# Turned blocks of a token mixer stored by row quarter first and channel chunk second

## The chip, the cores and the metric

The kernel runs on one core of a Trainium2 chip. The metric is the device time of one execution in microseconds (us), the median of several.

## The reference, cut to what matters

```python
def _attn_ref(x, weight):                       # x 8 x 4096 x 192, weight 8 heads x 7 taps
    w = softmax(weight)                         # over the taps
    out = np.einsum('hk,bskhg->bshg', w, x_unf) # causal convolution over 7 rows, per head
    return out.reshape(B, S, D)

def _moe_ref(x, w_tok1, w_tok2, w_ch1, w_ch2):
    xt = x.transpose(0, 2, 1)
    h = np.maximum(xt @ w_tok1, 0.0) @ w_tok2   # mixes the 4096 rows through 256
    u = x + h.transpose(0, 2, 1)
    h2 = np.maximum(u @ w_ch1, 0.0) @ w_ch2     # mixes the 192 channels through 1536
    return u + h2
```

All is float32. The kernel splits every float32 operand into a high and a low part (`hi`, `lo`) and multiplies high by high, high by low and low by high.

## The kernel before, in words

The eight batches are worked off in five groups: two single batches, then three pairs (`GROUPS`, L14). A group passes through two stages. The first (convolution, then the row mixer down to 256) runs as background work, in pieces that a planner puts between the instructions of the group ahead. The second takes eight tiles of 512 rows one after the other: `mix2` (L1030) mixes a tile's rows back up and adds, giving u; u is turned so that channels lie on partitions; `channel1` (matmuls in `channel1_mm`, L1214) multiplies by `w_ch1`, and `channel2` (L1290) by `w_ch2`, whose results two additions per 128 rows (L1304, L1305) take out of PSUM. For a pair, channel1 and channel2 run twice per tile, once for each batch of it.

The turning is what the change touches. VectorE's transpose (L1051 for a pair, L1044 for a single batch) turns blocks of 32 x 32 only, in place on the partitions. The other half of the work, bringing block (row quarter i, channel group q) to the partitions of q, is an exchange: `blocks_sent` issues sixteen DMAs (L1125) of 48 KB between two SBUF tiles, eight on SP's queue and eight on POOL's. Each goes from 32 partitions to 32 partitions. It is split by a channel dimension of three, `ND`, the chunks of 64 channels: a partition holds 12 blocks of 32 channels (6 for a single batch), numbered chunk first, then quarter.

What the exchange brings is then parted. For a pair, `parted` does so in this order, with c over the three chunks:

- ScalarE copies the arrived values to `own_hi` (L1157), which rounds them to the high part, and VectorE copies the lower 64 partitions of that over to the upper 64 of `swapped[0]` (L1158);
- VectorE subtracts: `own_lo` = arrived - `own_hi` (L1162), three times;
- ScalarE copies the lower 64 partitions of `own_lo` to the upper 64 of `swapped[1]` (L1165), three times;
- POOL sends the other halves by two DMAs (L1167).

`swapped[1]` is `other[:, 1]`, the very tile in which the arrived values lie, so L1165 overwrites what L1162 reads:

```python
        swapped = other[:, 0], other[:, 1]                          # L1152
            v = f32(other[:, 1, c]).rearrange("p (i j e) -> p j i e", i=NQ, e=QB)
            nc.vector.tensor_tensor(out=lo, in0=v, in1=f32(hi), op=ALU.subtract)
            nc.scalar.copy(out=swapped[1][high, c], in_=f32(own[1][low, c]))
```

The first block of channel1 is 18 matmuls, 9 products for each half of the array: three with the high weights and high values, three with the low weights and high values, three with the high weights and low values. In each triple one product per chunk c. The upper half's last three read `swapped[1]`, chunk by chunk. For a single batch, `parted_single` has one copy (L1135) and one subtraction in place (L1141) per chunk, and no swapped tile.

There are 29 exchanges: 5 for the second single batch (tile `own_lo`), 12 in the middle of the run for pairs (into `other` from `own_hi`, here called the open ones: the next tile's channel1 comes right after the channel2 under which they run) and 12 later ones for pairs (from the tile `raw`), which are issued one channel1 and channel2 earlier and here called the early ones.

Order: SP and POOL each issue their DMAs strictly in the program's order, and a framework adds waits on semaphores where two instructions touch the same bytes. Loads of the input for the convolution (L726, 128 partitions x 14 pieces of 384 bytes, 672 KB each) stand on SP's queue as well.

Of the kernel before, what the change touches and what calls it, by code (L numbers as in the profile page):

```python
# [148 lines left out]
def conv_mixer_kernel(ctx: ExitStack, tc: tile.TileContext, x, weight, w_tok1, w_tok2, w_ch1, w_ch2, out):  # L149
    nc = tc.nc  # L150
    B, S, D = x.shape
# [24 lines left out]
    def f32(ap):  # L176
        return ap.bitcast(F32)
# [829 lines left out]
    def mix2(gi, q, t2, u, z):  # L1007
# [15 lines left out]
        for step, js in enumerate(SHARES):  # L1023
            for j in js:
                if step < 2:
                    pss[j] = ps_x.tile([P, TT], F32, name="ps_x")
            for i, (kc, r, v, m) in enumerate(prods):
                for k, j in enumerate(js):
                    ks = half_rows(k)
                    nc.tensor.matmul(  # L1030
                        out=pss[j][:, :m], lhsT=lhs(kc, r, j)[ks], rhs=v[ks], start=step < 2 and i == 0,
                        stop=step > 1 and i == len(prods) - 1,
                    )
            if step < 2:
                part_ends(pss[js[1]])
            bg.fg(570 if nb == 1 else 1060, 0 if step < 2 else 1320 if nb == 1 else 900, 200 if z is None or step < 2 else -1e6)
            for j in sorted(js) if step > 1 else ():
                ps = pss[j]
                if nb == 1:
                    two, one = flat(u)[:, j, 0], flat(u)[:, j, 1]  # L1040
                    nc.vector.tensor_tensor(out=one, in0=ps[:, D:2 * D], in1=one, op=ALU.add)
                    nc.vector.tensor_tensor(out=two, in0=ps[:, :D], in1=one, op=ALU.add)
                    if z is not None:
                        nc.vector.transpose(  # L1044
                            out=z[:, :D // QB, j * QB:(j + 1) * QB], in_=two.rearrange("p (n e) -> p n e", e=QB)
                        )
                        bg.dve += 380
                else:
                    v = ps[:, :W].rearrange("p (b c d) -> p c b d", b=nb, d=D2)
                    nc.vector.tensor_tensor(out=u[:, j], in0=v, in1=u[:, j], op=ALU.add)  # L1050
                    nc.vector.transpose(  # L1051
                        out=z[:, :, j * QB:(j + 1) * QB],
                        in_=u[:, j].rearrange("p c b d -> p (c b d)").rearrange("p (n e) -> p n e", e=QB),
                    )
                    bg.dve += 580

# [20 lines left out]
    def transposed_halves(u, abc):  # L1077
# [28 lines left out]

        return {(1, 5): lambda: turn(0), (2, 3): parts}

    def blocks_sent(z, nb, pool, name):

        if nb == 1:
            other = own_tile("lo")
            blocks = z[:, :D // QB].rearrange("p (c n) t -> p n c t", n=NQ // 2)
            home = other
        else:
            other = pool.tile([P, 2, ND, TT], F32R, name=name)
            blocks = z.rearrange("p (c n) t -> p n c t", n=NQ)
            home = other[:, 1]  # L1120
        for k in range(NQ):
            for q in range(NQ):
                i = (q + k) % NQ
                queue = nc.gpsimd if q % 2 else nc.sync
                queue.dma_start(  # L1125
                    out=f32(home[q * QB:(q + 1) * QB, :, i * P:(i + 1) * P]),
                    in_=blocks[i * QB:(i + 1) * QB, q % (2 * nb)],
                )
        return other

    def parted_single(lo):
        own = own_tile("hi")
        for c in range(ND):
            v = f32(lo[:, c])
            nc.scalar.copy(  # L1135
                out=own[:, c].rearrange("p (j i e) -> p j i e", i=NQ, e=QB),
                in_=v.rearrange("p (i j e) -> p j i e", i=NQ, e=QB),
            )
            bg.fg(0, 700, 0)
            blocks = "p (i j e) -> p i j e"  # L1140
            nc.vector.tensor_tensor(  # L1141
                out=lo[:, c].rearrange(blocks, i=NQ, e=QB), in0=v.rearrange(blocks, i=NQ, e=QB),
                in1=f32(own[:, c]).rearrange("p (j i e) -> p i j e", i=NQ, e=QB), op=ALU.subtract,
            )
        own = own, lo.rearrange("p c (i j e) -> p c j i e", i=NQ, e=QB), range(ND)
        return [(own, own)]

    def parted(other):
# [3 lines left out]
        swapped = other[:, 0], other[:, 1]  # L1152
        low, high = slice(0, D2), slice(D2, P)
        for c in range(ND):
            v = f32(other[:, 1, c]).rearrange("p (i j e) -> p j i e", i=NQ, e=QB)
            hi, lo = (o[:, c].rearrange("p (j i e) -> p j i e", i=NQ, e=QB) for o in own)
            nc.scalar.copy(out=hi, in_=v)  # L1157
            nc.vector.tensor_copy(out=swapped[0][high, c], in_=f32(own[0][low, c]))  # L1158
        for c in range(ND):
            v = f32(other[:, 1, c]).rearrange("p (i j e) -> p j i e", i=NQ, e=QB)  # L1160
            hi, lo = (o[:, c].rearrange("p (j i e) -> p j i e", i=NQ, e=QB) for o in own)
            nc.vector.tensor_tensor(out=lo, in0=v, in1=f32(hi), op=ALU.subtract)  # L1162
        bg.dve += 3600
# [429 lines left out]
```

## Time and profile before

| | |
|---|---|
| three runs | 2046.98, 2049.78, 2050.49 us, median 2049.78 |
| the profiled execution, its own time | 2046.99 us |
| its span, first to last instruction | 2045.2 us |
| TensorE (PE) busy | 2018.5 us, 99% of the span |
| VectorE (DVE), ScalarE (ACT), GpSimd (POOL) busy | 68%, 38%, 11% |
| mean granted TensorE clock | 0.997 of full speed |
| the 16 DMA engines | 128 GB/s on average |

A busy share counts a matmul that stands in the pipeline behind a late operand as busy, so the 99% says that TensorE is never left for long, not that every product comes at its own pace. The pace is read from the starts of matmuls in the timeline.

### The profile page before, as it was taken

How to read it: one execution, taken by the hardware profiler on the slowest of the kernel's cores; microseconds unless marked ns; L12 is line 12 of the kernel's file. 1: busy time of each engine (PE TensorE's matmuls, PEld its weight loads, DVE VectorE, ACT ScalarE, POOL GpSimd, SP SyncE). 2: the span in 40 equal slices, each digit the busy share in tenths (PEclk: the TensorE clock that was granted, in tenths of full speed). 3: DMA queues.
4: the chain of work that ended last, by engine and by line, in shares of the span. 5: the costliest groups of instructions: out<-in, count | busy, mean ns of one | idle time of the engine just before them, and what ended most of it. 6: DMA issues, size and time to landing. Idle time of an engine off the chain costs nothing.

```text
span 2045.2 us, 52230 instructions
## 1 busy us (share of the span) xinstructions
PE 2018.5 (99%) x22404; PEld 1896.1 (93%) x22404; DVE 1398.0 (68%) x2747; ACT 782.5 (38%) x1582; POOL 219.1 (11%) x385
## 2 busy tenths in 40 slices
PE   9999999999999999999999999999999999999999
PEld 9889999998989889999998999899999999999998
DVE  8888989888758978847965895544455444554443
ACT  5677534433333434323333342322333223333222
POOL 0000000021211011101111101111110111101110
PEclk9999999999999999999999999999999999999999
DMA  9956445656455676436664375332332333323320
GB/s 303 311 159 206 138 131 177 174 142 191 140 143 133 174 181 158 106 100 138 168 161 116 92 186 138 84 79 54 74 80 72 83 84 76 79 73 84 79 53 16
DMA packets 285238, 262.67 MB, mean 128 GB/s; under 512 B 189136, under 2 KB 233040, under 8 KB 285008
## 3 DMA queue, kind: packets, MB, share of 16 engines
q1 hardware_dynamic: 263280, 185.27, 33.9%
q0 software_dynamic: 21728, 74.08, 12.7%
q8 instruction: 176, 2.88, 0.6%
q14 instruction: 54, 0.44, 0.1%
HBM read 146.31 MB, written 71.30 MB: 106 GB/s over the span
## 4 chain that ended last, share of the span: by engine, by line
PE 80%; DVE 7%; DMA 6%; ACT 3%; SPq 2%; issue 1%; POOL 1%; DVEq 0%; ACTq 0%; POOLq 0%
PE ps_x L1214 35%; PE ps_x L1290 31%; PE ps_x L1030 6%; PE ps_a L861 5%; DVE xc L738 2%; SPq L1125 2%; PE ps_x L1246 1%; DMA dec_raw<-in_moe_w_tok_dram 1%; DMA other<-own_hi 1%; DMA raw<-in_x_dram 1%; DVE hl L1273 1%; DVE own_lo L1162 1%; ACT own_hi L1157 1%; DMA dec_raw<-in_moe_w_ch_dram 1%; POOL other L1125 1%
## 5 line engine op out<-in xcount | busy, mean ns | idle before, releaser
L1290 PE MATMUL ps_x<-w,hh 64*128 64x384 f32 x5856 | 861.5, 356 | 0.3 <-DVE hl L1273 0.3
L1290 PE MATMUL ps_x<-w,hl 64*128 64x192 f32 x5856 | 831.9, 247 | 0.9 <-DVE hl L1273 0.8
L1290 PEld LDWEIGHTS ps_x<-w,hl 64*128 64x128 f32 x5856 | 696.2, 188 | 1.7 <-DVE hl L1273 1.4
L1290 PEld LDWEIGHTS ps_x<-w,hh 64*128 64x128 f32 x5856 | 691.9, 184 | 1.5 <-DVE hl L1273 0.8
L1272 ACT ACTIVATE hh<-ps_x 128x512 fp32r<-128x512 f32 x744 | 404.1, 594 | 551.7 <-PE ps_x L1214 551.5
L1273 DVE SCALAR_TENSOR_TENSOR hl<-ps_x,hh 128x512 fp32r<-128x512 f32 x744 | 477.0, 685 | 196.3 <-ACT hh L1272 195.5
L738 DVE SCALAR_TENSOR_TENSOR xc<-raw,cw,xc 128x384 f32<-128x384 f32 (+1 forms) x768 | 383.1, 562 | 14.4 <-ACT xc L736 14.3
L1214 PE MATMUL ps_x<-other,w_hi 64*128 64x512 f32 x1296 | 353.4, 393 | 3.7 <-ACT other L1165 1.2
L1214 PE MATMUL ps_x<-own_hi,w_hi 64*128 64x512 f32 x1440 | 342.4, 398 | 7.2 <-ACT own_hi L1135 6.2
L1214 PE MATMUL ps_x<-own_lo,w_hi 64*128 64x512 f32 x1440 | 336.9, 393 | 0.0
L1214 PE MATMUL ps_x<-own_hi,w_lo 64*128 64x512 f32 x1440 | 332.6, 390 | 0.0
L1214 PEld LDWEIGHTS ps_x<-other,w_hi 64*128 64x128 f32 x1296 | 235.0, 184 | 36.7 <-ACT other L1165 12.5
L1304 DVE TENSOR_TENSOR osb<-ps_x,u 128x192 f32<-128x192 f32 x244 | 85.6, 351 | 241.8 <-PE ps_x L1290 241.8
L1214 PEld LDWEIGHTS ps_x<-own_lo,w_hi 64*128 64x128 f32 x1440 | 222.1, 185 | 20.0 <-DVE own_lo L1162 1.2
L1214 PEld LDWEIGHTS ps_x<-own_hi,w_lo 64*128 64x128 f32 x1440 | 222.6, 186 | 18.1
L1214 PEld LDWEIGHTS ps_x<-own_hi,w_hi 64*128 64x128 f32 x1440 | 215.7, 186 | 25.3 <-ACT own_hi L1135 7.7
L1214 PE MATMUL ps_x<-other,w_lo 64*128 64x512 f32 x648 | 182.8, 388 | 0.0
L423 ACT COPY ps_x<-seen 1x2 f32<-1x2 f32 x198 | 30.0, 152 | 365.0 <-PE ps_x L1290 315.3
L1030 PE MATMUL ps_x<-h,t 64*128 64x384 f32 (+1 forms) x1408 | 134.2, 327 | 2.2 <-DVE hl L1273 1.6
L1030 PEld LDWEIGHTS ps_x<-h,t 64*128 64x128 f32 x1408 | 127.6, 184 | 5.5 <-DVE hl L1273 3.4
L1214 PEld LDWEIGHTS ps_x<-other,w_lo 64*128 64x128 f32 x648 | 119.4, 184 | 10.7
L861 PE MATMUL ps_a<-xhl,t 64*128 64x384 f32 x1056 | 120.8, 336 | 2.7 <-DMA t<-t1p 2.7
(178 smaller groups left out, 1834.6 us busy)
## 6 DMA issues: line engine op xcount, KB each, us to landing
raw<-in_x_dram SPq DMA_DIRECT2D x56, 672.0 KB, 8.6
t<-t2d SPq DMA_DIRECT2D x64, 512.0 KB, 5.8
u<-xcd SPq DMA_DIRECT2D x62, 384.0 KB, 7.7
xcd<-xc POOLq DMA_DIRECT2D x28, 768.0 KB, 7.9
t<-t1p SPq DMA_DIRECT2D x32, 512.0 KB, 5.0
out_dram<-osb POOLq DMA_DIRECT2D x34, 384.0 KB, 2.7
out_dram<-osb SPq DMA_DIRECT2D x29, 384.0 KB, 2.8
t2d<-stage SPq DMA_DIRECT2D x16, 512.0 KB, 4.6
```

The lines of the kernel that those rows point to most:

```text
L423: nc.scalar.copy(out=ps[0:1, TT - 2:TT], in_=seen)
L738: nc.vector.scalar_tensor_tensor(out=dst, in0=src, scalar=cw[:, h, k:k + 1], in1=dst, op0=ALU.mult, op1=ALU.add)
L861: nc.tensor.matmul(out=accs[kcs[k]][:, :nb * D], lhsT=w[ks], rhs=x[ks], start=first and step == 0 and i == 0, stop=last and step == 1 and ...
L1030: nc.tensor.matmul(out=pss[j][:, :m], lhsT=lhs(kc, r, j)[ks], rhs=v[ks], start=step < 2 and i == 0, stop=step > 1 and i == len(prods) - 1,)
L1125: queue.dma_start(out=f32(home[q * QB:(q + 1) * QB, :, i * P:(i + 1) * P]), in_=blocks[i * QB:(i + 1) * QB, q % (2 * nb)],)
L1157: nc.scalar.copy(out=hi, in_=v)
L1162: nc.vector.tensor_tensor(out=lo, in0=v, in1=f32(hi), op=ALU.subtract)
L1214: nc.tensor.matmul(out=ps, lhsT=w1[w][rows, t[h][2][c], p * P:(p + 1) * P], rhs=t[h][v][rows, c], start=a and n == 0, stop=z and n == len( ...
L1272: nc.scalar.activation(out=h["hh", f], in_=ps, func=AF.Relu)
L1273: nc.vector.scalar_tensor_tensor(out=h["hl", f], in0=ps, scalar=0.0, in1=f32(h["hh", f]), op0=ALU.max, op1=ALU.subtract)
L1290: nc.tensor.matmul(out=pss[j][:, :m], lhsT=h[part, f][ks, j * P:(j + 1) * P], rhs=w2[ks, f, :m], start=step < 2 and n == 0 and part == "hh ...
L1304: nc.vector.tensor_tensor(out=rows(osb[:, j]), in0=rows(ps[:, :D]), in1=tokens(u, i)[:, j], op=ALU.add)
```

## The change

The turned blocks are numbered quarter first, then chunk, so that the three chunks of one block pair lie next to each other, both in the tile that is sent and in the tile that arrives. A transfer thus has one run of 1536 bytes per partition in place of three of 512. All readers and writers of these tiles use views (`by_rows`, `by_blocks_of`) that follow the new numbering: the transposes, ScalarE's copies to the high part, and the subtractions. What `swapped[1]` means is not changed: chunk c at columns 512c to 512c + 511.

```diff
@@ -1042,15 +1042,16 @@
                     nc.vector.tensor_tensor(out=two, in0=ps[:, :D], in1=one, op=ALU.add)
                     if z is not None:
                         nc.vector.transpose(
-                            out=z[:, :D // QB, j * QB:(j + 1) * QB], in_=two.rearrange("p (n e) -> p n e", e=QB)
+                            out=by_rows(z, 1)[:, :, :, j * QB:(j + 1) * QB],
+                            in_=two.rearrange("p (c q e) -> p c q e", c=ND, e=QB),
                         )
                         bg.dve += 380
                 else:
                     v = ps[:, :W].rearrange("p (b c d) -> p c b d", b=nb, d=D2)
                     nc.vector.tensor_tensor(out=u[:, j], in0=v, in1=u[:, j], op=ALU.add)
                     nc.vector.transpose(
-                        out=z[:, :, j * QB:(j + 1) * QB],
-                        in_=u[:, j].rearrange("p c b d -> p (c b d)").rearrange("p (n e) -> p n e", e=QB),
+                        out=by_rows(z, nb)[:, :, :, j * QB:(j + 1) * QB],
+                        in_=u[:, j].rearrange("p c b d -> p c (b d)").rearrange("p c (q e) -> p c q e", e=QB),
                     )
                     bg.dve += 580
 
@@ -1106,43 +1107,47 @@
 
         return {(1, 5): lambda: turn(0), (2, 3): parts}
 
+    def by_rows(z, nb):
+        return z[:, :nb * D // QB].rearrange("p (q c) t -> p c q t", c=ND)
+
+    def by_blocks_of(t):
+        return t.rearrange("p c t -> p (c t)").rearrange("p (i c t) -> p i c t", i=NQ, c=ND)
+
     def blocks_sent(z, nb, pool, name):
 
 
 
         if nb == 1:
             other = own_tile("lo")
-            blocks = z[:, :D // QB].rearrange("p (c n) t -> p n c t", n=NQ // 2)
             home = other
         else:
             other = pool.tile([P, 2, ND, TT], F32R, name=name)
-            blocks = z.rearrange("p (c n) t -> p n c t", n=NQ)
             home = other[:, 1]
+        blocks = z[:, :nb * D // QB].rearrange("p (q c) t -> p q (c t)", c=ND)
+        home = home.rearrange("p c t -> p (c t)").rearrange("p (i n) -> p i n", i=NQ)
         for k in range(NQ):
             for q in range(NQ):
                 i = (q + k) % NQ
                 queue = nc.gpsimd if q % 2 else nc.sync
                 queue.dma_start(
-                    out=f32(home[q * QB:(q + 1) * QB, :, i * P:(i + 1) * P]),
+                    out=f32(home[q * QB:(q + 1) * QB, i]),
                     in_=blocks[i * QB:(i + 1) * QB, q % (2 * nb)],
                 )
         return other
 
     def parted_single(lo):
-        own = own_tile("hi")
+        own, blocks = own_tile("hi"), by_blocks_of(lo)
         for c in range(ND):
-            v = f32(lo[:, c])
+            v = f32(blocks[:, :, c])
             nc.scalar.copy(
-                out=own[:, c].rearrange("p (j i e) -> p j i e", i=NQ, e=QB),
-                in_=v.rearrange("p (i j e) -> p j i e", i=NQ, e=QB),
+                out=own[:, c].rearrange("p (j i e) -> p i j e", i=NQ, e=QB), in_=v.rearrange("p i (j e) -> p i j e", e=QB)
             )
             bg.fg(0, 700, 0)
-            blocks = "p (i j e) -> p i j e"
             nc.vector.tensor_tensor(
-                out=lo[:, c].rearrange(blocks, i=NQ, e=QB), in0=v.rearrange(blocks, i=NQ, e=QB),
+                out=blocks[:, :, c].rearrange("p i (j e) -> p i j e", e=QB), in0=v.rearrange("p i (j e) -> p i j e", e=QB),
                 in1=f32(own[:, c]).rearrange("p (j i e) -> p i j e", i=NQ, e=QB), op=ALU.subtract,
             )
-        own = own, lo.rearrange("p c (i j e) -> p c j i e", i=NQ, e=QB), range(ND)
+        own = own, blocks.rearrange("p i c (j e) -> p c j i e", e=QB), range(ND)
         return [(own, own)]
 
     def parted(other):
@@ -1152,12 +1157,12 @@
         swapped = other[:, 0], other[:, 1]
         low, high = slice(0, D2), slice(D2, P)
         for c in range(ND):
-            v = f32(other[:, 1, c]).rearrange("p (i j e) -> p j i e", i=NQ, e=QB)
+            v = f32(by_blocks_of(other[:, 1])[:, :, c]).rearrange("p i (j e) -> p j i e", e=QB)
             hi, lo = (o[:, c].rearrange("p (j i e) -> p j i e", i=NQ, e=QB) for o in own)
             nc.scalar.copy(out=hi, in_=v)
             nc.vector.tensor_copy(out=swapped[0][high, c], in_=f32(own[0][low, c]))
         for c in range(ND):
-            v = f32(other[:, 1, c]).rearrange("p (i j e) -> p j i e", i=NQ, e=QB)
+            v = f32(by_blocks_of(other[:, 1])[:, :, c]).rearrange("p i (j e) -> p j i e", e=QB)
             hi, lo = (o[:, c].rearrange("p (j i e) -> p j i e", i=NQ, e=QB) for o in own)
             nc.vector.tensor_tensor(out=lo, in0=v, in1=f32(hi), op=ALU.subtract)
         bg.dve += 3600
```

The order of the instructions on every engine is the same as before. Two places show what moves. The first is ScalarE's queue at the first open exchange, with what each instruction waits for: the copies to `own_hi` (L1157, L1162 in the change), the copies of `own_lo` into `other` (L1165, L1170 in the change), then channel1's activations (L1272, L1277). Before:

```order
L423 COPY ps_x<-seen 1x2 [waits DVE_49,PE_49] x4
L1157 CAST own_hi<-other 128x512 [waits DMAHW0_49,DMASW7_49,DMAHW1_49,DMASW6_49,DMAHW2_49,DMASW5_49,DMAHW3_49,DMASW4_49,DMAHW4_49,DMASW3_49,DMAHW5_49,DMASW2_49,DMAHW6_49,DMASW1_49,DMAHW7_49,DMASW0_49,DVE_49]
L1157 CAST own_hi<-other 128x512 x2
L1165 CAST other<-own_lo 64x512 [waits DVE_49,Activation_49] x3
L1272 ACTIVATE hh_8659<-ps_x 128x512 [waits PE_49] x4
```

And in the change:

```order
L423 COPY ps_x<-seen 1x2 [waits DVE_49,PE_49] x4
L1162 CAST own_hi<-other 128x512 [waits DMAHW0_49,DMASW7_49,DMAHW1_49,DMASW6_49,DMAHW2_49,DMASW5_49,DMAHW3_49,DMASW4_49,DMAHW4_49,DMASW3_49,DMAHW5_49,DMASW2_49,DMAHW6_49,DMASW1_49,DMAHW7_49,DMASW0_49,DVE_49]
L1162 CAST own_hi<-other 128x512 x2
L1170 CAST other<-own_lo 64x512 [waits DVE_49,Activation_49]
L1170 CAST other<-own_lo 64x512 x2
L1277 ACTIVATE hh_8659<-ps_x 128x512 [waits PE_49] x4
```

Before, each of the three copies has a wait of its own for VectorE; now the first waits for VectorE once and the two behind it wait for nothing more, so the first one's wait covers them all.

The second place is SP's queue at the two open exchanges that start at 978.97 and 1036.28 us in the trace. Before:

```order
L1125 DMA other<-own_hi 32x3x128 x8
L726 DMA raw_13404<-in_x_dram 128x14x96 x2
L726 DMA raw_13409<-in_x_dram 128x14x96 x2
L1336 DMA out_dram<-osb 128x768
L978 DMA t_13487<-t2d 128x2x512 x2
L988 DMA u<-xcd_77 128x12x64 x2
L1125 DMA other<-own_hi 32x3x128 x8
L726 DMA raw_14285<-in_x_dram 128x14x96 x2
```

And in the change:

```order
L1132 DMA other<-own_hi 32x384 x8
L726 DMA raw_13404<-in_x_dram 128x14x96 x2
L726 DMA raw_13409<-in_x_dram 128x14x96 x2
L1341 DMA out_dram<-osb 128x768
L978 DMA t_13487<-t2d 128x2x512 x2
L988 DMA u<-xcd_77 128x12x64 x2
L1132 DMA other<-own_hi 32x384 x8
L726 DMA raw_14285<-in_x_dram 128x14x96 x2
```

Nothing changes places; the exchange's DMAs have two dimensions in place of three. Input loads stand right behind the exchange on SP's queue here, as at seven of the twelve open exchanges; at four an output store stands there, at one a load of `t1p`.

## Rows read from the trace of the kernel before

**Rows 1.** The page: the span, TensorE's busy time, and by 40 equal slices the granted TensorE clock in tenths.

```profile
span 2045.2 us, 52230 instructions
PE 2018.5 (99%) x22404; PEld 1896.1 (93%) x22404; DVE 1398.0 (68%) x2747; ACT 782.5 (38%) x1582; POOL 219.1 (11%) x385
PEclk9999999999999999999999999999999999999999
```

**Rows 2.** Busy time by stretch (us from the span's start: length, then PE, PEld, DVE, ACT and POOL busy with instructions, granted clock, DMA share, GB/s): the open exchanges and the early ones.

```profile
590.00:1320.00 730.00, 722.62 (x8145) 667.35 (x8143) 543.38 (x1037) 258.69 (x538) 90.62 (x155) 1.00 0.54 138
1331.00:1990.00 659.00, 659.00 (x7632) 630.11 (x7630) 328.28 (x635) 200.97 (x420) 72.22 (x132) 1.00 0.30 75
```

**Rows 3.** Groups of instructions by line, with busy us and mean ns, then the idle time of the engine before them by releaser.

```profile
L1165 ACT CAST other<-own_lo 64x512 fp32r<-64x512 f32 x54 | 32.8, 618 | 31.2 <-DVE own_lo L1162 31.2
L1157 ACT CAST own_hi<-other 128x512 fp32r<-128x512 f32 x54 | 29.9, 620 | 46.0 <-DMA other<-own_hi 46.0
...
L1162 DVE TENSOR_TENSOR own_lo<-xc,own_hi 128x512 fp32r<-128x512 f32 x18 | 11.4, 687 | 2.2 <-issue 2.2
...
L1157 ACT CAST own_hi<-xc 128x512 fp32r<-128x512 f32 x18 | 10.0, 627 | 0.0
```

**Rows 4.** ScalarE's copies into `swapped[1]` (L1165): who waited for them, in us and times.

```profile
  PEld ps_x L1214: 12.5, 30
  PE ps_x L1214: 1.2, 6
```

**Rows 5.** Timeline of ScalarE from 1043 us, the open exchange issued at 1036: start, length, line, operation, count, in brackets the idle time before and its releaser.

```profile
1043.80 1.66 ACT L1157 CAST own_hi<-other 128x512 fp32r<-128x512 f32 x3 [4.00 <-DMA other<-own_hi]
1047.04 1.82 ACT L1165 CAST other<-own_lo 64x512 fp32r<-64x512 f32 x3 [1.58 <-DVE own_lo L1162]
```

**Rows 6.** The same stretch on VectorE.

```profile
1046.25 1.90 DVE L1162 TENSOR_TENSOR own_lo<-other,own_hi 128x512 fp32r<-128x512 f32 x3 [0.34 <-DMA raw<-in_x_dram]
...
1049.11 0.36 DVE L1305 TENSOR_TENSOR osb<-ps_x,osb 128x192 f32<-128x192 f32 x1
```

**Rows 7.** The same stretch on TensorE: the first block of channel1 and the start of the second. Rows with `other` are the upper half of the array, with `own` the lower.

```profile
1046.06 0.41 PE L1214 MATMUL ps_x<-own_hi,w_hi 64*128 64x512 f32 x1
...
1047.22 0.39 PE L1214 MATMUL ps_x<-other,w_lo 64*128 64x512 f32 x1
...
1047.44 0.39 PE L1214 MATMUL ps_x<-other,w_lo 64*128 64x512 f32 x1
...
1047.71 0.50 PE L1214 MATMUL ps_x<-other,w_hi 64*128 64x512 f32 x1
...
1048.31 0.50 PE L1214 MATMUL ps_x<-other,w_hi 64*128 64x512 f32 x1
...
1048.91 0.50 PE L1214 MATMUL ps_x<-other,w_hi 64*128 64x512 f32 x1
1049.01 0.46 PE L1214 MATMUL ps_x<-own_hi,w_hi 64*128 64x512 f32 x1
1049.52 0.50 PE L1214 MATMUL ps_x<-other,w_hi 64*128 64x512 f32 x1
1049.53 0.50 PE L1214 MATMUL ps_x<-own_hi,w_hi 64*128 64x512 f32 x1
1049.86 0.39 PE L1214 MATMUL ps_x<-other,w_hi 64*128 64x512 f32 x1
```

**Rows 8.** Timelines of SP's and POOL's queues, the open exchange at 1036 (input loads behind it) and the one at 1093 (none behind it), and when ScalarE starts on the latter.

```profile
1036.28 5.08 SPq L1125 DMA_DIRECT2D other<-own_hi  x8
1041.46 1.49 SPq L726 DMA_DIRECT2D raw<-in_x_dram  x2
...
1036.85 4.35 POOL L1125 DMA_DIRECT2D other<-own_hi  x8 [17.37 <-DVE xc L738]
...
1093.78 5.10 SPq L1125 DMA_DIRECT2D other<-own_hi  x8
...
1094.35 4.35 POOL L1125 DMA_DIRECT2D other<-own_hi  x8 [18.31 <-ACT ps_x L423]
...
1101.10 1.14 ACT L1157 CAST own_hi<-other 128x512 fp32r<-128x512 f32 x2 [3.79 <-DMA other<-own_hi]
```

**Rows 9.** The exchange's DMAs (L1125) from 1093 to 1101 us: issue durations in ns (min/median/max), and us from the start of the issue to the landing.

```profile
L1125 SPq DMA_DIRECT2D other<-own_hi x8: 591/598/604, 1093.8 to 1098.3; - x8
L1125 POOL DMA_DIRECT2D other<-own_hi x8: 548/548/573, 1094.3 to 1098.2; - x8
...
DMA to landing us min/median/max: 1.9/2.1/2.4
```

**Rows 10.** Issue durations in ns of DMAs with one run per partition: two kinds on SP, one on POOL.

```profile
L1336 SPq DMA_DIRECT2D out_dram<-osb x33: 332/357/10315, 424.5 to 2042.6; - x33
...
L1439 SPq DMA_DIRECT2D t2d<-stage x16: 319/328/2213, 111.2 to 248.5; - x16
...
L1167 POOL DMA_DIRECT2D other<-own_lo x18: 517/523/530, 608.1 to 1981.8; - x18
```

**Rows 11.** Landings of the exchange's DMAs (L1125) from 444 to 457 us: an exchange of a single batch that was issued while two input loads (issued from 440.7 us) were in flight.

```profile
DMA to landing us min/median/max: 3.7/5.5/8.2
```

**Rows 12.** TensorE's waits: engine and line, releaser, us in total, times, longest.

```profile
PE ps_x L1214 <- ACT own_hi L1135: 6.2, 2, 4.5
```

**Rows 13.** An early exchange: its issue on SP (L1125), ScalarE's copies after it, and TensorE's first product that reads it.

```profile
1335.16 5.11 SPq L1125 DMA_DIRECT2D xc<-raw  x8
...
1361.86 1.82 ACT L1165 CAST xc<-own_lo 64x512 fp32r<-64x512 f32 x3 [1.60 <-DVE own_lo L1162]
...
1371.28 0.41 PE L1214 MATMUL ps_x<-xc,w_hi 64*128 64x512 f32 x1
```

**Rows 14.** Groups by line again: VectorE's subtraction with plain views (L1273), and the transposes of the open exchanges.

```profile
L1273 DVE SCALAR_TENSOR_TENSOR hl<-ps_x,hh 128x512 fp32r<-128x512 f32 x744 | 477.0, 685 | 196.3 <-ACT hh L1272 195.5
...
L1051 DVE STREAM_TRANSPOSE own_hi<-u 128x384 f32<-128x384 f32 x48 | 27.8, 579 | 1.6
```

## The prediction

> **What bounds the kernel now.** TensorE does: busy for 2018.5 of 2045.2 us at the full clock [rows 1], and without any gap over the stretch of the early exchanges [rows 2]. A change elsewhere therefore counts only where TensorE waits, or keeps time because an operand is late. The groups by line show where that is at the exchanges. Before the copies to `own_hi` (L1157) of the open exchanges ScalarE sits idle for 46.0 us, and the DMAs end it; before those of the early ones it sits idle for 0.0 [rows 3]. So only the open exchanges arrive when they are already wanted. Who waits at their end is told by the view of L1165: 30 weight loads and 6 matmuls [rows 4], 36 in all, which is 12 open exchanges times 3 chunks. At every open exchange, each of the three copies into `swapped[1]` is what TensorE's next product waits for.
>
> The waits add up to 13.7 us only because a matmul that is held in the pipeline counts as busy. The timeline shows the real loss; I take the exchange of 1036 us. The arrived data start ScalarE at 1043.80, the copies L1165 run from 1047.04 to 1048.86 [rows 5], the subtractions before them from 1046.25 [rows 6], and the upper half's last three products start at 1047.71, 1048.31 and 1048.91 [rows 7], 0.60 apart like the copies, each 0.05 after its copy's end. Undisturbed products are 0.22 to 0.23 apart (1047.22, 1047.44) [rows 7]. Nine of them from 1046.06 would end at 1048.1. Instead the second block's first product starts at 1049.01, and its upper half at 1049.52, held by the PSUM buffer that L1305 frees at 1049.47 [rows 6]. The chain is thus: landing, L1157, the swap of the high part, the subtractions L1162, and then L1165 and L1305 side by side.
>
> **The change part by part.**
>
> *The copies L1165 wait longer.* They write columns 512c to 512c + 511 of `other[:, 1]`. Before, these were just what the subtraction of chunk c had read. Now chunk c's blocks lie in all four quarters, so the first 512 columns hold blocks of all three chunks, and the first copy may start only after the third subtraction; the moved wait in ScalarE's queue says the same. Today the first copy starts 0.10 after its own subtraction's end (three of them take 1.90 from 1046.25, spaced 0.60, so the first ends near 1046.94) [rows 5, 6]. After the change it starts 0.10 after the third's end at 1048.15, at 1048.25: 1.21 later. All three copies move by 1.21, and the upper half's last product from 1048.91 to 1050.12. The second block then starts at 1050.22. Its wait for L1305 is over by then, which gives part back: its second upper product comes at 1050.60 (0.23 and the 0.15 by which upper trails lower) in place of 1049.86 [rows 7]. That leaves 0.74 us. Behind the copies on ScalarE stand channel1's activations, which wait for this same block, so nothing else is delayed. Twelve open exchanges: **+8.9 us**. The rest of the run gives TensorE no slack to take it up [rows 2].
>
> *The exchange itself.* It moves the same bytes. What can get shorter is the issue. On SP eight DMAs take 5.1 us [rows 8], 0.598 each [rows 9]; DMAs with one run per partition take 0.328 to 0.357 [rows 10], though these have 128 partitions, not 32. I take 0.33, with 0.60 as the other end. SP is then done 2.9 us after its first issue in place of 5.1. POOL does not follow: 0.548 now [rows 9], 0.523 for the nearest kind [rows 10], 0.2 us over eight. Its last issue ends at 1098.70 at the exchange of 1093, with ScalarE's start 2.40 later [rows 8]. The shortest landing is 1.9 from the start of the issue [rows 9], 1.35 from its end; today the last landing, 2.4 after 1098.3, precedes ScalarE's start at 1101.10 by 0.4. So the start could come 2.40 - 1.35 - 0.4 = 0.65, with POOL's 0.2 some 0.8 us earlier. Bounds: nothing and -0.8. I take the middle, -0.4, as POOL remains the last. For the five open exchanges without input loads right behind them: **-2.0 us** (0 to -4.0).
>
> *Input loads come closer.* At the other seven they stand right behind the exchange on SP, start right after it (1041.46 against 1036.28 + 5.08) [rows 8], and would start 2.2 us earlier, while POOL still issues its last three or four DMAs. Such loads hold POOL's transfers up: with two in flight the sixteen transfers landed after 5.5 at the median [rows 11], without after 2.1 [rows 9]. So each of the seven lies between -0.8 (no effect) and +3.4 (the full difference). Only the last few of POOL's eight are met, and the loads need a moment to fill the engines; I take +0.3, near the lower end: **+2.1 us** (-5.6 to +23.8).
>
> The Trainium skill, page "DMA: Bandwidth & Descriptors", section "Queues, rings and completion order", says that each DMA engine goes round the queues that have work and changes after every packet. By that rule POOL would lose a packet's time per turn and the seven would gain like the five, -2.8 in place of +2.1. The landings under input loads [rows 11] do not agree with so small a loss.
>
> *Single batches.* Their subtraction stays in place chunk by chunk, and no copy follows. Two of five hold TensorE, 6.2 us together [rows 12]; these are the ones issued under input loads [rows 11], whose end decides. Bounds 0 and -6.2; I take -0.75 each, about two of SP's shorter issues plus a little: **-1.5 us**.
>
> *Early exchanges.* Issue at 1335.16, copies done at 1363.68, first use at 1371.28 [rows 13]. The later copies use up 1.2 of 7.6 us: nothing. If that cover went, each would cost what an open one costs.
>
> *New views* in transposes, copies and subtractions: the subtraction with four-dimensional views takes 0.687 [rows 3], with plain ones 0.685 [rows 14], and runs of 32 values stay runs of 32. Nothing for the transposes at 0.579 [rows 14] either; a tenth more on each of four would add 0.23 per open exchange.
>
> **Sum:** 8.9 - 2.0 + 2.1 - 1.5 = +7.5 us. Against the profiled execution, 2046.99, that is 2054.5. The median of the runs shown, 2049.78, stands 2.8 higher, and with it the forecast is 2057.3. What a measurement can tell from no change here is 0.2%, 4.1 us.
>
> **The rivals.**
>
> *A. The earlier landing wins: faster.* If SP's issue falls to a half and neither POOL nor the input loads hold the last transfers, the landing comes early at all twelve. With s us gained at the single batches it decides from a gain per open exchange of 0.74 + (4.1 - s) / 12: 0.96 for s = 1.5, 0.57 for the bound s = 6.2. At both bounds: 12 x (0.74 - 0.8) - 6.2 = -6.9, 2042.9. For it: ScalarE's 46.0 us of idle time [rows 3]. Against it: POOL's eight issues, which the change hardly touches.
>
> *B. It cancels.* A gain of 0.6 at each open exchange, inside the bound of 0.8, if input loads cost POOL's transfers nothing, and 2 at the single ones: 12 x (0.74 - 0.6) - 2 = -0.3, 2049.5. The Trainium skill's rule above would have it so. For it: the bounds allow it. Against it: [rows 11].
>
> *C. Input loads overrun POOL's half.* +2.5 at each of seven: 8.9 - 2.0 + 17.5 - 1.5 = +22.9, 2072.7. For it: [rows 11]. Against it: only the tail of the issue is met.
>
> *D. The transfers don't get shorter at all*, because the issue's length hangs on the 32 partitions and not on the runs. Then landings stay, no load moves, and the longer wait stands alone: +8.9, 2058.7.
>
> **How the numbers follow.** The forecast, with terms inside their bounds, 0.45; A 0.10; B 0.18; C 0.12; D 0.15. Faster by over 0.2% is A: 0.10. Within it is B: 0.18. Slower holds the forecast, C and D: 0.72. The range leaves out A's far side and most of C: 2046 to 2068.
>
> **What would show it.** In the profile after: the first L1170 copy starts after the third subtraction's end, some 4.45 us after the first copy to `own_hi` in place of 3.24, and TensorE's last three upper products move with it; again 36 waits for it. SP's issue near 0.33, POOL's near 0.52. ScalarE's idle time before `own_hi` a little shorter at the five, not at the seven. The forecast is wrong if the copies still follow their own subtractions, or if the landings come more than 0.74 us earlier at most open exchanges.

## The result, and the profile after

The changed kernel takes 2059.51 us (median of 4 runs, 2058.03 to 2061.14), the kernel before 2049.49 (median of 4). The ratio is 1.0051 with an interval of 1.0034 to 1.0068: slower by about 10 us. The forecast was 2057.3. Its sum is nearly right. Its parts are not: the place where it put the loss pays for itself almost entirely, and most of the loss is where it put nothing.

The profiled execution took 2058.03 us, 11.0 more than that of before. The page (span, TensorE, granted clock by slices) looks as before [rows 1]:

```profile
span 2056.3 us, 52179 instructions
PE 2020.2 (98%) x22404; PEld 1908.9 (93%) x22404; DVE 1399.1 (68%) x2747; ACT 776.8 (38%) x1582; POOL 205.8 (10%) x385
PEclk9999999999999999999999999999999999999999
```

Groups by line of the copies and subtractions, lines L1170, L1162 and L1167 of the change (columns as in [rows 3]). They hold the tiles named `other`, which are the 12 open exchanges and six of the early ones; the other six early ones use `xc`:

```profile
L1170 ACT CAST other<-own_lo 64x512 fp32r<-64x512 f32 x54 | 29.8, 614 | 52.9 <-DVE own_lo L1167 52.9
L1162 ACT CAST own_hi<-other 128x512 fp32r<-128x512 f32 x54 | 29.9, 621 | 38.6 <-DMA other<-own_hi 38.6
L1167 DVE TENSOR_TENSOR own_lo<-other,own_hi 128x512 fp32r<-128x512 f32 x54 | 34.1, 687 | 6.0 <-issue 3.1 <-PE ps_x L1295 2.2 <-DMA raw<-in_x_dram 0.7
```

Two things move. ScalarE waits longer for the subtractions, 52.9 us in place of 31.2. The six early exchanges in this group have 16.9 of it (six times 2.81) in place of 9.6 (six times 1.60), so the open ones have 36.0 in place of 21.6. And it waits less for the exchange's DMAs, 38.6 in place of 46.0 [rows 3]: the landings come earlier.

TensorE's waits (engine and line, releaser: us in total, times, longest):

```profile
PEld ps_x L1219 <- ACT other L1170: 20.6, 36, 1.7
...
PEld ps_x L1295 <- ACT ps_x L423: 7.9, 12, 0.7
...
PE ps_x L1219 <- ACT own_hi L1142: 6.5, 2, 3.9
PE ps_x L1219 <- ACT other L1170: 5.9, 9, 1.4
...
PE ps_x L1295 <- ACT ps_x L423: 5.1, 12, 0.4
```

Each of the 36 copies into `swapped[1]` at the open exchanges now holds up a weight load (26.5 us with nine waits of matmuls). Before, it was 30 weight loads and six matmuls, 13.7 us [rows 4]; the six stand at exchanges where three weight loads wait for the same three copies, so 30 copies of the 36 were waited for, not all. New are the two rows of L423: twelve times channel2 (L1295) waits for the small copy L423, once in each early exchange. In the trace of before no such wait is found.

**An early exchange.** ScalarE at the first one: before (its row of L1165 stands in [rows 13]), and after.

```profile
1358.59 1.66 ACT L1157 CAST own_hi<-xc 128x512 fp32r<-128x512 f32 x3
...
1363.59 0.15 ACT L423 COPY ps_x<-seen 1x2 f32<-1x2 f32 x1
1364.65 0.15 ACT L423 COPY ps_x<-seen 1x2 f32<-1x2 f32 x1 [0.92 <-PE ps_x L1290]
```

```profile
1361.75 1.66 ACT L1162 CAST own_hi<-xc 128x512 fp32r<-128x512 f32 x3
1366.23 1.66 ACT L1170 CAST xc<-own_lo 64x512 fp32r<-64x512 f32 x3 [2.81 <-DVE own_lo L1167]
1367.79 0.24 ACT L423 COPY ps_x<-seen 1x2 f32<-1x2 f32 x2
```

And TensorE there, after the change:

```profile
1367.28 0.35 PE L1295 MATMUL ps_x<-w,hh 64*128 64x384 f32 x1
1367.30 0.42 PE L1295 MATMUL ps_x<-w,hl 64*128 64x192 f32 x2
1368.00 0.44 PE L1295 MATMUL ps_x<-w,hh 64*128 64x384 f32 x2 [0.27 <-ACT ps_x L423]
```

L423 writes two values into the PSUM buffer of channel2's first step once that step is done (`part_ends`); the third step goes on in the same buffer. It stands behind the three copies on ScalarE, and runs the moment they end. Before, that was 5.00 us after the first copy to `own_hi`, and the second L423, released by TensorE at the end of the second step, came 1.06 later: the first was done in time. After, it runs at 6.04, the second directly behind it with nothing left to wait for. The third step starts only at 1368.00, 0.70 after the product ahead of it where such pairs stand 0.1 to 0.2 apart. From SP's issue of the second early exchange to that of the last, ten tiles on, it is 562.27 us before and 568.99 after: 0.67 a tile, or **8.1 us for twelve**. From the first early issue to the end of the span it is 8.0.

The Trainium skill, page "PSUM — Partial Sum Buffer", section "Engine vs sequencer instructions", calls ScalarE's queue strictly first in, first out. The rows agree: L423 had nothing to wait for but its place.

**An open exchange.** The one issued at 1036 us before and at 1037 after. ScalarE:

```profile
1044.04 1.66 ACT L1162 CAST own_hi<-other 128x512 fp32r<-128x512 f32 x3 [3.35 <-DMA other<-own_hi]
1048.48 1.66 ACT L1170 CAST other<-own_lo 64x512 fp32r<-64x512 f32 x3 [2.78 <-DVE own_lo L1167]
```

TensorE, the upper half's last products of the first block and first two of the second:

```profile
1050.19 0.50 PE L1219 MATMUL ps_x<-other,w_hi 64*128 64x512 f32 x1
...
1050.29 0.47 PE L1219 MATMUL ps_x<-own_hi,w_hi 64*128 64x512 f32 x1
...
1050.53 0.39 PE L1219 MATMUL ps_x<-other,w_hi 64*128 64x512 f32 x1
...
1050.76 0.39 PE L1219 MATMUL ps_x<-other,w_hi 64*128 64x512 f32 x1
```

SP's and POOL's queues there:

```profile
1037.17 4.95 SPq L1132 DMA_DIRECT2D other<-own_hi  x8
1042.22 1.41 SPq L726 DMA_DIRECT2D raw<-in_x_dram  x2
...
1037.71 3.95 POOL L1132 DMA_DIRECT2D other<-own_hi  x8 [17.27 <-DVE xc L738]
```

The issue durations (min/median/max in ns) and landings of this exchange:

```profile
L1132 SPq DMA_DIRECT2D other<-own_hi x8: 513/588/590, 1037.2 to 1041.5; - x8
L1132 POOL DMA_DIRECT2D other<-own_hi x8: 496/496/532, 1037.7 to 1041.2; - x8
...
DMA to landing us min/median/max: 1.8/2.0/2.3
```

The copies start 4.44 after ScalarE's first, in place of 3.24 [rows 5]. The second block's second upper product comes 6.72 after that first copy, in place of 6.06 [rows 5, 7]: 0.66 lost. But ScalarE's first copy comes 6.87 after SP's first issue, in place of 7.52 [rows 5, 8]: 0.65 won. At the exchange without input loads behind it, issued at 1094.64 and taken up at 1101.44, it is 6.80 in place of 7.32 [rows 8]. SP's eight issues are hardly shorter (4.95 for 5.08), POOL's are (3.95 for 4.35). From the end of SP's issues to ScalarE's start it is 1.92 in place of 2.44, from the end of POOL's 2.38 in place of 2.60. Which queue's transfer lands last the rows don't say, so how much of the gain is issue and how much is flight stays open.

The same for all twelve open exchanges, from SP's first issue to ScalarE's first copy (us; the columns are the times of issue before, with a star where input loads stand behind the exchange on SP):

| | 594* | 653* | 721* | 790* | 855 | 922* | 979* | 1036* | 1094 | 1164 | 1237 | 1303 | sum |
|---|---|---|---|---|---|---|---|---|---|---|---|---|---|
| before | 8.97 | 8.36 | 9.02 | 7.22 | 8.14 | 7.11 | 7.32 | 7.52 | 7.32 | 7.33 | 7.97 | 8.13 | 94.4 |
| the change | 8.12 | 7.92 | 6.44 | 6.90 | 6.96 | 7.16 | 6.97 | 6.87 | 6.80 | 7.33 | 7.65 | 7.58 | 86.7 |

That is 7.7 us won, 5.1 at the seven with input loads and 2.6 at the five without. Seven exchanges win 0.3 to 0.65, three win more (0.85, 2.58 and 1.18), and two win nothing.

The whole stretch from the first open exchange (595.12) to the first early one (1338.27) is 743.15 us, before 740.68 (594.48 to 1335.16): +2.5. TensorE's clock took more than that. By stretch: length, TensorE's busy time, granted clock, DMA share, GB/s.

```profile
609.00:610.00 1.00, 0.98 (x5) 0.62 0.99 162
610.00:612.00 2.00, 2.00 (x12) 0.50 1.30 186
612.00:613.00 1.00, 1.00 (x8) 0.67 1.26 272
...
1121.00:1122.00 1.00, 1.00 (x11) 0.62 0.10 37
1122.00:1125.00 3.00, 3.00 (x26) 0.56 0.01 4
```

Twice it fell to the lower of its two levels (1.2 of 2.4 GHz), for 1.7 us of lost work each time (the length times the part of the clock that was not granted), 3.4 together. Without them the stretch would be 739.7, which is 0.9 less than before. The first fall comes after TensorE had waited at the exchange of 595 (busy for 0.94 us of the two from 606.00), the second after a wait outside the exchanges (0.83 us of the three from 1118.00). The trace of before has that second wait as well (0.89 of three), and no fall there or elsewhere in the stretch.

### The profile page after: what moved, and what is told of

Same layout as the page of the kernel before. It is cut to its first block, busy times and chain, and to the rows that moved or that the text cites. A ratio compares the mean times of both kernels' runs of the same rounds, so it can differ in the third digit from the quotient of the medians.

```text
span 2056.3 us, 52179 instructions
## 1 busy us (share of the span) xinstructions
PE 2020.2 (98%) x22404; PEld 1908.9 (93%) x22404; DVE 1399.1 (68%) x2747; ACT 776.8 (38%) x1582; POOL 205.8 (10%) x385
## 4 chain that ended last, share of the span: by engine, by line
PE 78%; DVE 8%; DMA 4%; ACT 4%; SPq 3%; issue 2%; DVEq 0%; POOL 0%; ACTq 0%
PE ps_x L1219 36%; PE ps_x L1295 28%; PE ps_x L1030 6%; PE ps_a L861 5%; SPq L1132 3%; DVE xc L738 2%; DVE own_lo L1167 2%; DVE hl L1278 1%; DMA raw<-in_x_dram 1%; PE ps_x L1251 1%; DMA other<-own_hi 1%; ACT other L1170 1%; DMA early_raw<-in_moe_w_tok_dram 1%; ACT own_hi L1162 1%; DMA t<-t1p 1%
## 5 line engine op out<-in xcount | busy, mean ns | idle before, releaser
L1295 PE MATMUL ps_x<-w,hh 64*128 64x384 f32 x5856 | 855.8, 357 | 5.4 <-ACT ps_x L423 5.1
L1295 PE MATMUL ps_x<-w,hl 64*128 64x192 f32 x5856 | 788.2, 247 | 0.9 <-DVE hl L1278 0.8
L1295 PEld LDWEIGHTS ps_x<-w,hh 64*128 64x128 f32 x5856 | 680.0, 184 | 9.4 <-ACT ps_x L423 7.9
L1295 PEld LDWEIGHTS ps_x<-w,hl 64*128 64x128 f32 x5856 | 683.6, 188 | 1.9 <-DVE hl L1278 1.4
L1277 ACT ACTIVATE hh<-ps_x 128x512 fp32r<-128x512 f32 x744 | 403.3, 594 | 560.9 <-PE ps_x L1219 560.0
L423 ACT COPY ps_x<-seen 1x2 f32<-1x2 f32 x198 | 29.3, 152 | 350.7 <-PE ps_x L1295 303.8
```

Of the source, the lines that this page charges most:

```text
L423: nc.scalar.copy(out=ps[0:1, TT - 2:TT], in_=seen)
L1277: nc.scalar.activation(out=h["hh", f], in_=ps, func=AF.Relu)
L1295: nc.tensor.matmul(out=pss[j][:, :m], lhsT=h[part, f][ks, j * P:(j + 1) * P], rhs=w2[ks, f, :m], start=step < 2 and n == 0 and part == "hh ...
```

## The experiments

All stand against the kernel before, which was run beside them: 2048.44 us (21 runs) beside the first four, 2049.15 (24 runs) beside the rest.

**The wait alone.** The kernel before, with a dependency added (the diffs here are shortened):

```diff
-            nc.scalar.copy(out=swapped[1][high, c], in_=f32(own[1][low, c]))
+            copy = nc.scalar.copy(out=swapped[1][high, c], in_=f32(own[1][low, c]))
+            if c == 0:      # ins: the third subtraction
+                tc.add_manual_dep(copy.ins, ins.ins.name, DependencyInfo(Sync, DATA), reason="wait")
```

> The kernel before, with nothing but the longer wait: the first of the three copies into swapped[1] also waits for the third subtraction. Theory T (the wait is paid twice): +0.74 us at each of 12 open exchanges, as TensorE's last three upper products come later, and +0.65 at each of 12 early ones, since the copies hold up the small copy L423 behind them on ScalarE, for which channel2's third step waits: 2049.5 + 8.9 + 7.8 = 2066. Rival P (the prediction's step): +8.9 at the open ones, nothing at the early ones: 2058.4. Rival Q (the open exchanges have slack, landings play no part): the same as the changed kernel, 2059.5.

Measured: 2071.05, ratio 1.0113 (1.0100 to 1.0127), +22.6. The early tiles cost what they cost in the change (568.94 for ten). ScalarE at the exchange that the change has at 1037:

```profile
1054.27 1.66 ACT L1157 CAST own_hi<-other 128x512 fp32r<-128x512 f32 x3 [3.97 <-DMA other<-own_hi]
1058.70 1.66 ACT L1165 CAST other<-own_lo 64x512 fp32r<-64x512 f32 x3 [2.78 <-DVE own_lo L1162]
```

TensorE's second upper product of the second block:

```profile
1060.98 0.39 PE L1219 MATMUL ps_x<-other,w_hi 64*128 64x512 f32 x1
```

It comes 6.71 after the first copy: the same loss of 0.65. The open stretch is longer by 13.4 us, and four falls of the clock are in it, three of them behind late open exchanges:

```profile
611.00:615.00 4.00, 4.00 (x24) 0.59 1.14 201
...
672.00:676.00 4.00, 4.00 (x24) 0.57 0.87 226
...
740.00:744.00 4.00, 3.72 (x16) 0.57 1.18 222
...
1133.00:1137.00 4.00, 4.00 (x36) 0.57 0.01 3
```

At 0.57 to 0.59 over 4 us, each costs 1.6 to 1.7, 6.8 together. What is left, 6.6, is near 12 x 0.65 = 7.8. So theory T holds with a size too small, and P and Q fall: the wait is paid at the open exchanges and at the early ones, and three falls of the clock behind late open exchanges come on top. ScalarE's idle time before `own_hi` is 46.3 here: without the new numbering the landings stay.

**The wait taken out.** The changed kernel, with the low parts kept in the same numbering as what arrives, so that copy c overwrites only what subtraction c has read:

```diff
+        mine, theirs = by_blocks_of(own[1]), by_blocks_of(other[:, 1])
...
-            nc.scalar.copy(out=swapped[1][high, c], in_=f32(own[1][low, c]))
+            nc.scalar.copy(out=theirs[high, :, c], in_=f32(mine[low, :, c]))
...
+        los = [t.rearrange("p i c (j e) -> p c j i e", e=QB) for t in (mine, theirs)]
```

> The changed kernel, with own_lo and swapped[1] also kept by quarter and chunk, so that each copy into swapped[1] overwrites only what its own subtraction has read, and waits for that one alone. Theory T: both costs of the wait go, the earlier landing stays (some 0.45 us at each of 12 open exchanges, transposes' end to ScalarE's start 0.5 shorter): 2049.5 - 5.4 = 2044. Rival U (the loss of 0.67 per tile in the early stretch has another cause, such as the new views): 2044 + 8 = 2052. Rival V (the landing gain is noise): 2049.5.

Measured: 2046.85 (11 runs, 2044.81 to 2052.59), ratio 0.9994 (0.9985 to 1.0003). The copies start 3.24 after the first copy again, and the landings stay early:

```profile
1043.85 1.66 ACT L1163 CAST own_hi<-other 128x512 fp32r<-128x512 f32 x3 [3.41 <-DMA other<-own_hi]
1047.09 1.82 ACT L1173 CAST other<-own_lo 64x512 fp32r<-64x512 f32 x3 [1.58 <-DVE own_lo L1168]
```

TensorE waits 8.1 + 0.4 us for them (26.5 in the change), and never for L423 in channel2. The open stretch is 736.79, 3.9 less than before, with one fall of the clock in it. But ten early tiles take 564.80, 0.25 a tile more than before, with no wait to account for it; what is new there is that TensorE reads the low parts through a strided view. The time alone lies between T's 2044 and V's 2049.5, and its interval doesn't exclude V's "no gain"; the trace does, as the twelve waits from issue to first copy add up to 86.6 us here too (94.4 before). U falls. T holds for both costs of the wait and for the landings, and missed this price.

**L423 ahead of the copies.** The changed kernel; at the early exchanges the copies into `swapped[1]` are issued after channel2's first step:

```diff
-                    abc = parted(other)
+                    later = []
+                    made = abc = parted(other, later)   # L1170 and L1172 go into later
+                    between[0, NF - 1] = later[0]       # after part_ends of step 0
```

> The changed kernel, with one thing moved, at the 12 early exchanges alone: on ScalarE the first small copy L423 of channel2 stands ahead of the three copies into swapped[1] (and the two DMAs behind them), not behind. Theory T: the early stretch gets its 8.0 us back, the rest stays: 2059.5 - 8.0 = 2051.5. Rival U (the early loss does not come from L423): 2059.5.

Measured: 2052.06 (11 runs), ratio 1.0019 (1.0010 to 1.0028): 3.6 us above the kernel before that ran beside it, where the change stood 10.0 above its own, so some 6.4 us are won back. ScalarE at the first early exchange:

```profile
1361.95 1.66 ACT L1162 CAST own_hi<-xc 128x512 fp32r<-128x512 f32 x3
1364.52 0.15 ACT L423 COPY ps_x<-seen 1x2 f32<-1x2 f32 x1 [0.91 <-PE ps_x L1302]
1366.42 1.66 ACT L1172 CAST xc<-own_lo 64x512 fp32r<-64x512 f32 x3 [1.74 <-DVE own_lo L1167]
```

The copies come as late as in the change, L423 slips into the wait, and ten early tiles take 562.26, as before. That the early loss hangs on L423's place is shown. What is left lies ahead of the early exchanges: in this trace 1.4 before the first open exchange and 1.9 in the open stretch, which has the change's two falls of the clock (3.4) again.

**L423 ahead of the copies, in the kernel before.** The same edit.

> The kernel before, with the small copy L423 ahead of the three copies into swapped[1] at the early exchanges. Theory T: before the change L423 ended about 0.7 us before channel2's third step wanted it, so nothing: 2048.4 within 1.5. Rival (L423 cost something already before): faster by up to 4.

Measured: 2048.10 (11 runs), ratio 0.9993 (0.9984 to 1.0002): nothing, as T has it; ten early tiles take 562.27. L423's place did no harm until the copies ahead of it came later.

**The pairs alone.** The change without its five single exchanges (their lines as before).

> The change for the pairs alone: the five exchanges of single batches keep chunk-first numbering and runs of 512 bytes. Theory T: the single exchanges neither gain nor lose more than the scatter of their input loads, 2059.5 within 1. The prediction's term: they gain 1.5 by the change, so 2061.0 without it.

Measured: 2057.95 (5 runs), ratio 1.0054 (1.0041 to 1.0067), against 1.0051 for the whole change. The intervals overlap, and a gain of 1.5 can't be told from none; there is no sign of it, as the two exposed singles hold TensorE for 6.5 us in the change, for 6.8 in this run and for 6.2 before [rows 12].

**One end alone.** In the first run only the sent tile is renumbered, in the second only the tile that arrives:

```diff
-            blocks = z.rearrange("p (c n) t -> p n c t", n=NQ)        # the first
+        blocks = z[:, :nb * D // QB].rearrange("p (q c) t -> p q c t", c=ND)
-            home = other[:, 1]                                        # the second
+        home = by_blocks_of(home)
```

> Only the tile that is sent is numbered quarter first; the tile that arrives keeps chunk first, so that a transfer reads one run of 1536 bytes per partition and writes three of 512, and each copy into swapped[1] waits for its own subtraction alone, as before. Theory T1 (a transfer gets cheaper only where both ends are one run): landings stay, 2048.4. Rival T2 (the run that is read decides): landings come 0.7 us earlier at 12 open exchanges and nothing is paid for it: 2048.4 - 8.4 = 2040.

> The mirror of the run before it: only the tile that arrives is numbered quarter first, so a transfer reads three runs of 512 bytes and writes one of 1536, and the first copy into swapped[1] waits for the third subtraction. Theory T1: landings stay as before the change and the wait is paid in full, 2066 to 2071 as with the wait alone. Rival T3 (the run that is written decides): as the changed kernel, 2059.5.

Measured: 2048.69 (11 runs), ratio 0.9997 (0.9989 to 1.0006); and 2070.60 (4 runs), ratio 1.0106 (1.0090 to 1.0121). T1 holds in both: an end alone brings no time. At ten of the twelve open exchanges the landings stay within 0.3 us in both runs; the third comes 2.0 earlier in both (and the first 0.6 in the second run), for which no run shows the cause. So some 2 of the 2.58 us that the change wins at the third need not come from runs that are whole at both ends. The packets of SP's queue during the exchange at about 1094 (packets, MB, share) in the change, then with the sent tile alone, then with the arriving tile alone:

```profile
q1 hardware_dynamic: 384, 0.39, 19.3%
```

```profile
q1 hardware_dynamic: 896, 0.39, 23.1%
```

```profile
q1 hardware_dynamic: 896, 0.39, 23.2%
```

Before it was 896 as well: 112 for each of eight transfers, now 48. POOL's queue has 256 packets in all four, and only its issue got shorter (496 ns for 548, 548 and 547). SP's packets and POOL's issue changed in the same kernels, so which of them brings how much of the earlier landing stays open.

The Trainium skill, page "DMA: Bandwidth & Descriptors", section "Why a DMA increments its semaphore by 16 and not by 1", says that a descriptor moves one contiguous run; SP's counts agree, and show that both ends must be one run. Its section "Why small descriptors are slow (HBM only)" says that transfers between SBUF and SBUF don't suffer from short ones. No run here settles that: with longer runs seven of the twelve exchanges are taken up 0.3 to 0.65 us earlier, but POOL's shorter issue can account for up to 0.40 of it.

**Both remedies, each where it is cheap.** At the open exchanges the low parts numbered as they arrive, at the early ones plain tiles with L423 ahead of the copies.

> The changed kernel with both remedies, each where it is cheap: at the open exchanges own_lo and swapped[1] by quarter and chunk, so that each copy waits for its own subtraction; at the early ones plain tiles and L423 ahead of the copies. Theory T: the open stretch as in the run that had the first remedy everywhere, the early stretch without the 0.25 us per tile that TensorE lost there to the strided operand: 2046.9 - 3.0 = 2043.9. Rival (that loss came from somewhere else): 2046.9.

Measured: 2045.36 (8 runs, 2041.54 to 2046.56), ratio 0.9978 (0.9967 to 0.9988): faster than the kernel before by 3.8 us, than the change by 14. Ten early tiles take 562.27, so the 0.25 a tile goes with the low parts' numbering. TensorE's products that read `own_lo` there, first with the strided view everywhere (the wait taken out), then here (busy us, mean ns):

```profile
L1223 PE MATMUL ps_x<-own_lo,w_hi 64*128 64x512 f32 x360 | 103.5, 394 | 0.0
```

```profile
L1250 PE MATMUL ps_x<-own_lo,w_hi 64*128 64x512 f32 x360 | 101.6, 388 | 0.0
```

The open stretch is 735.38, 5.3 less than before. What the new layout brings is thus real; the change lost it, and more, to one dependency.

The two stretches side by side (starts of SP's issues; the trace of each profiled execution). "Lost to the clock" adds up the part of the clock that was not granted, microsecond by microsecond:

| | first open to first early | lost to the clock | without that | ten early tiles |
|---|---|---|---|---|
| before | 740.68 | 0 | 740.7 | 562.27 |
| the change | 743.15 | 3.4 | 739.7 | 568.99 |
| the wait alone | 754.09 | 6.8 | 747.3 | 568.94 |
| the wait taken out | 736.79 | 1.7 | 735.1 | 564.80 |
| L423 ahead, in the change | 742.60 | 3.4 | 739.2 | 562.26 |
| L423 ahead, before | 741.05 | 0 | 741.1 | 562.27 |
| the pairs alone | 743.75 | 3.4 | 740.3 | 569.06 |
| sent tile alone | 741.81 | 3.4 | 738.4 | 562.26 |
| arriving tile alone | 748.30 | 3.4 | 744.9 | 568.99 |
| both remedies | 735.38 | 0 | 735.4 | 562.27 |

The last column repeats to 0.1 us. The first scatters with the falls of the clock and a few late landings, and each row is one execution. Without the falls, kernels that differ only in the early part or at the single batches stand 0.4 apart (before) and 1.1 apart (the change), and the two with the wait and old landings 2.4, as the third exchange of one lands 2 us earlier. A fall right behind a late open exchange stands in five of the ten traces, the five with the longer wait. The fall near 1121 stands in seven, with the longer wait and without.

## Why the prediction was right in its sum and wrong in its parts

*The copies L1165, +8.9.* Right in mechanism and nearly in size: first copy at 4.44 (4.45 foreseen), and 0.66 in place of 0.74 at the exchange of 1037, so an estimated +7.9 for twelve; the wait alone cost 6.6 there without the clock. The 36 waits before were read as 36 copies, and were 30. Not foreseen was the clock, at 1.7 us for each fall and 3.4 in all.

*The exchange itself and the input loads, -2.0 and +2.1.* The first came near its size by another way, the second did not occur. SP's issue was taken at 0.33 and came at 0.588; the other end, 0.60, was right, and the 32 partitions were the better guide (rival D, in this point). POOL's fell to 0.496, below the 0.523 taken. With SP's issue as long as ever, the input loads start 5.05 us after the exchange's first issue (5.18 before), when POOL is through: they came no closer. Rival C's overrun had no occasion either, and neither the term of +2.1 nor the rule on queues taking turns, weighed against it, was put to the test. The five exchanges without input loads won 2.6 us (2.0 foreseen), the seven with them won 5.1 where 2.1 of loss was foreseen. The gain of one exchange was bounded at 0.8: nine keep to that, three do not (0.85, 1.18 and 2.58), and the forecast has no term for these. That is fewer than the "most" by which it would have called itself wrong. In all the landings gave -7.7 where the two terms together gave +0.1. So the open exchanges came out at +7.9 - 7.7 = +0.2, with the clock's 3.4 on top (+2.5 in the trace), in place of +9.0.

*Early exchanges, 0.* This step failed. It said that "the later copies use up 1.2 of 7.6 us: nothing". The 7.6 us lie between the copies and the product that reads them, and that cover did hold. But another instruction was behind the copies on ScalarE: L423, for which channel2 waits. The text looked behind the copies only at the open exchanges ("Behind the copies on ScalarE stand channel1's activations"), where L423 runs ahead of them. Measured: 0.67 a tile, 8.1 in all; with that one copy moved, ten early tiles take 562.26 again.

*Single batches, -1.5.* No sign of it. *New views, 0.* Right: the subtractions take 0.687 as before [rows 3].

The sum, +7.5 foreseen and +11.0 between the profiled executions, is early +8.0, open +2.5 and +0.6 ahead of the first open exchange (595.12 for 594.48, a start that scatters by 6 us over the ten traces). It came close by luck: a loss left out was as large as a gain left out.

Rival B had the open exchanges best: a gain of some 0.6 at each (0.64 on average here) that nearly cancels the wait. Its 2 us at the single batches did not show, and the early loss, which it left out as well, kept the time from cancelling. Rival A asked for 0.74 + 4.1 / 12 = 1.08 for each open exchange with nothing won at the single ones, and did not get it. Moving L423 alone still leaves the kernel slower than before; only where the wait at the open exchanges is gone too, as in the last experiment, do the landings win.

## What to carry to other kernels

When a wait gets longer on an in-order engine, list what stands behind the waiting instruction at every place where it runs, not only at the one that seems exposed, and ask for each who waits for it; a cover between an instruction and its reader says nothing of its neighbours in the queue. A buffer that is overwritten while it is read can be handed over piece by piece only as long as both sides cut it alike: a new numbering of one side turned a chunk-by-chunk handover into a wait for all chunks here. And a sum that comes out right is no proof of its terms; compare the stretches one by one.

## What was not expected of the hardware

- Transfers between two SBUF tiles from 32 to 32 partitions are issued on SP in 588 ns with one run per partition and in 597 with three, while POOL goes from 548 to 496. The landing comes earlier by more than the issues get shorter at the exchange of 1037 (0.65 for 0.13 on SP and 0.40 on POOL); what makes the rest is open.
- TensorE's granted clock fell to its lower level behind gaps of little more than a microsecond (1.41 us of idle time ahead of a product at 670.37 with the wait alone, the fall from 672), for 1.6 to 1.7 us of lost work a time. But a gap does not always bring one: in the change 1.41 us ahead of a product at 608.35 did and 1.40 at 668.37 did not, and near 1120 a gap of 2.17 us in the change did where one of 2.71 in the trace of before did not.
- A matmul that reads its moving operand in runs of 32 values, as the low parts did where the wait was taken out, costs hardly more, but not nothing: 394 ns on average in place of 388, and 0.25 us per tile of two channel1 passes.
